# Moving a sign extraction from VectorE to ScalarE in the weight conversion of a fused attention and MLP kernel

## The chip, the cores and the metric

The kernel runs on one core of a Trainium2 chip. The core has TensorE (PE, matmuls and transposes into PSUM), VectorE (DVE), ScalarE (ACT), GpSimd (POOL) and SyncE (SP, which issues the DMAs here). The metric is the device time of one execution in microseconds (us).

## The reference

Three stages run one after another. A linear attention over 8 batches and 8 heads (576 positions, head size 64), then two MLPs over the 4608 resulting tokens of width 512:

```python
k_s = softmax(k, axis=2); q_s = softmax(q, axis=-1)
x = (q_s @ (k_s^T @ v)) as [4608, 512]
g = x @ w_gate; x = (silu(g) * (x @ w_val)) @ w_out      # hidden size 1536
h = x @ w_in;   x = elu(h) @ w_out2                       # hidden size 2048
```

The weights come as float64, the activations as float32.

## The kernel before, in words

Tokens are worked on in nine blocks of 512. Phase "a" runs the first MLP on one half of its hidden tiles (f, six tiles of 128) for all nine blocks, phase "b" on the other half, phase "2" runs the second MLP. During phase "a" the attention of the block after next is spread over the steps of the current block by hand-written plans (PLAN0, PLAN1, PLAN: name, then the pass f and step s at which it is issued). There is no reordering by a scheduler: every engine executes its instructions in the order in which the program issues them.

Every product is made of three matmuls over split operands: a high part and a low part of the weights and of the activations (mm3, proj). One pass over a hidden tile in phases "a" and "b" is gate (12 matmuls into a PSUM bank "a"), value (12 into the other bank "a"), and 12 matmuls of the output product of the pass before. Between them ACT computes parts of silu (L660 to L663), DVE multiplies (L667, L670, L673), ACT writes the high part of the result (L645) and DVE or POOL the low part (L651). There are two banks "a", so the gate of the next pass needs L670 of this one to have read its bank. In phase "2" the bank is freed by L688.

The weights arrive as the bits of float64 numbers, in 68 chunks of [128, 512]. Each chunk goes through four stages, each with a counter in `stage`:

- load (L125, L127): SP loads the 64-bit words into a raw buffer (three buffers, nine chunks at the start by borrowing two others).
- scale (`conv_scale`, L139): ACT reads the upper 32-bit word as a float32, multiplies by 2^-112 and writes cg (three buffers).
- bits (`conv_bits`): DVE makes the bits of a float32 from cg and the lower word. L154 shifts cg left by 3 and clears the sign, into a PSUM tile c; L157 takes the sign bit of cg and ORs it in; L161 ORs the top three bits of the lower word in and writes cd (four buffers).
- split (`conv_split`): ACT copies cd as the high part of the weight (L182), POOL subtracts to get the low part (L183). Twenty weight slots in a ring hold the result until the last block has used it.

`conv()` issues one step of each stage in the order split, bits, scale, load, load. It is called three times per pass in block ("a", 0), once per step in block ("a", 1) until 18 chunks are split, twice per pass in the last block of phases "a" and "b", otherwise once per pass or not at all where the ring is full. `limit` holds the loader at 18 chunks until late in phase "a". Three chunks are converted in `first_block` before the passes begin.

Names that the steps below use: km is the key maximum (L270 to L273 on DVE), transposed by PE at L280 and L293; ke the shifted and exponentiated keys (L310, L312, then ACT L315, L316), read by PE at L331; q is shifted on POOL at L360 and normalised at L378 in block 0, transposed at L390, copied by ACT at L398 and multiplied at L451; L299 is an ACT copy of the broadcast key maximum.

Of the kernel before, what the change touches and what calls it, by code (L numbers as in the profile page):

```python
# [7 lines left out]
FP32 = mybir.dt.float32  # L8
F32R = mybir.dt.float32r
U32 = mybir.dt.uint32  # L10
I64 = mybir.dt.int64
ACTF = mybir.ActivationFunctionType
ALU = mybir.AluOpType
AX = mybir.AxisListType
# [3 lines left out]
def kernel(  # L18
# [23 lines left out]
    nc = tc.nc  # L42
# [9 lines left out]
    NW1, NW2, NRAW, NCG, NCD = 20, 12, 3, 3, 4  # L52
# [5 lines left out]
    cv_p = ctx.enter_context(tc.tile_pool(name="cv", bufs=2))  # L58
# [43 lines left out]
    stage = {"load": 0, "scale": 0, "bits": 0, "split": 0}  # L102
    raws, gs, ds, loaded, calls, free = {}, {}, {}, {}, [0], [0]
# [5 lines left out]
    def early_raws():  # L109
        t = x_p.tile([128, 4, 512], I64, tag="x", name="xraw")  # L110
        u = ev_p.tile([128, 2, 512], I64, tag="ev", name="evraw")
        for n in range(6):
            early[NRAW + n] = t[:, n] if n < 4 else u[:, n - 4]

    def conv_load():
# [6 lines left out]
        _, src, cols = chunks[n]  # L122
        t = early.pop(n) if n in early else raw_p.tile([128, 512], I64, tag="raw", name="raw")
        if cols:
# [7 lines left out]

    def conv_scale(wait=0):
        n = stage["scale"]
        if n >= stage["load"] or n >= stage["bits"] + NCG or calls[0] < loaded[n] + wait:
            return
        stage["scale"] += 1
        g = cv_p.tile([128, 512], U32, tag="cg", name="cg", bufs=NCG)
        nc.scalar.activation(  # L139
            out=g.bitcast(FP32), in_=raws[n][:, :, 1].bitcast(FP32), func=ACTF.Copy,  # L140
            scale=2.0 ** -112,
        )
        gs[n] = g

    def conv_bits():
        n = stage["bits"]
        if n >= stage["scale"] or n >= free[0] + NCD:
            return  # L150
        stage["bits"] += 1
        g = gs.pop(n)
        s = ps_c.tile([128, 512], U32, tag="c", name="c")
        nc.vector.tensor_scalar(  # L154
            s, g, 3, 0x7FFFFFFF, op0=ALU.logical_shift_left, op1=ALU.bitwise_and
        )
        nc.vector.scalar_tensor_tensor(  # L157
            out=s, in0=g, scalar=0x80000000, in1=s, op0=ALU.bitwise_and, op1=ALU.bitwise_or
        )
        d = cv_p.tile([128, 512], U32, tag="cd", name="cd", bufs=NCD)  # L160
        nc.vector.scalar_tensor_tensor(  # L161
            out=d, in0=raws.pop(n)[:, :, 0], scalar=29, in1=s,
            op0=ALU.logical_shift_right, op1=ALU.bitwise_or,
        )
        ds[n] = d

    def conv_split(eng):
        n = stage["split"]
# [12 lines left out]
        df = ds.pop(n).bitcast(FP32)  # L181
        nc.scalar.activation(out=w[:, 0, :], in_=df, func=ACTF.Copy)  # L182
        eng.tensor_tensor(w[:, 1, :], df, w[:, 0, :].bitcast(FP32), op=ALU.subtract)  # L183
# [3 lines left out]
    def conv(eng=None, wait=2):  # L187
        calls[0] += 1
        free[0] = stage["split"]
        conv_split(eng or nc.gpsimd)  # L190
        conv_bits()
        conv_scale(wait)
        conv_load()
        conv_load()
# [94 lines left out]
    def k2(b):  # L289
# [7 lines left out]
        if b == 1:  # L297
            mb = at1.tile([128, H, D], FP32, tag="km", name="mb")
            nc.scalar.activation(out=mb, in_=m, func=ACTF.Copy)  # L299
            km_t[b] = mb  # L300
# [13 lines left out]
    def kexp(b):  # L314
        nc.scalar.activation(out=ke[:, 0:4], in_=ke[:, 0:4], func=ACTF.Exp)  # L315
        nc.scalar.activation(out=ke[0:NREST, 4], in_=ke[0:NREST, 4], func=ACTF.Exp)  # L316

# [44 lines left out]
    def qexp(t, n):  # L362
        x = q_t[t][:, 4 * n:4 * n + 4]
        nc.scalar.activation(out=x, in_=x, func=ACTF.Exp)

# [105 lines left out]
    def first_block():  # L471
# [103 lines left out]
        qexp(0, 1)  # L575
        qnorm(0, 0, nc.gpsimd)
        conv_scale()
        conv_scale()
        kv(0, 0, 1)
        qT(0, 0)  # L580
        qT(0, 2)
        qsum(0, 1)
        qnorm(0, 1, nc.gpsimd)
        kv(0, 1, 1)
        conv_bits()
        conv_split(nc.gpsimd)
        qT(0, 1)
# [5 lines left out]
        load_q(1)  # L593
        xT(0, 2, 0)
        conv_bits()
        conv_split(nc.gpsimd)
        xT(0, 2, 1)
# [340 lines left out]
    with tc.manual_schedule():  # L938
        nc.gpsimd.memset(ident, 1.0)
        nc.gpsimd.affine_select(  # L940
            out=ident, in_=ident, pattern=[[-1, 128]], compare_op=ALU.is_equal, fill=0.0,
# [39 lines left out]
```

## Time and profile before

| what | value |
|---|---|
| median of 3 runs | 1791.45 us (1791.27 to 1791.88) |
| the profiled execution's own time | 1792.23 us |
| its span, first to last instruction | 1790.5 us |
| PE busy | 1752.0 us, 98% |
| DVE busy | 924.9 us, 52% |
| ACT busy | 856.0 us, 48% |
| POOL busy | 173.1 us, 10% |
| mean granted clock of TensorE | 0.995 |

The busy shares are means over stages with different limits. "Idle before" in a row is the time for which the engine stood still just before that instruction, and "<-" names what ended it. Times in a timeline are counted from the span's start.

### The profile page before, as it was taken

The page shows a single profiled execution, that of the slowest core. Times are in us where ns is not written, and L with a number is a line of the kernel's source. Part 1 is how long each engine was busy: PE and PEld are TensorE (multiplying, and loading weights), DVE is VectorE, ACT ScalarE, POOL GpSimd, SP SyncE. Part 2 cuts the span into 40 slices and gives each one's busy share as a digit, 9 for nine tenths or more (in the row PEclk, how much of TensorE's full clock was granted, in tenths as well). Part 3 has the DMA queues.
Part 4 walks back from the last instruction along what each step waited for, and adds up shares of the span by engine and source line. Part 5 has one row for each costly group of instructions (what it writes and reads, how often), then busy time and mean ns, then how long its engine had stood idle before and what let it go on. Part 6 is the DMA issues. An engine that isn't in the chain of part 4 may idle for free.

```text
span 1790.5 us, 21046 instructions
## 1 busy us (share of the span) xinstructions
PE 1752.0 (98%) x8448; PEld 1433.3 (80%) x8448; DVE 924.9 (52%) x1383; ACT 856.0 (48%) x1466; POOL 173.1 (10%) x135
## 2 busy tenths in 40 slices
PE   6799999999999999999999999999999999999999
PEld 4577888888888888888888788888888888888887
DVE  6866567556577666534346744333433343334343
ACT  4563544534465454433334654444444444444444
POOL 3630000000022222111113300000000000000000
PEclk9899999999999999999999999999999999999999
DMA  9274534341255344433334401010101010101000
GB/s 273 80 228 102 147 100 124 105 114 65 78 192 176 129 171 168 165 118 118 118 118 164 174 3 71 1 71 1 71 1 71 1 71 1 71 1 71 1 24 24
DMA packets 103106, 169.13 MB, mean 94 GB/s; under 512 B 41696, under 2 KB 80608, under 8 KB 98528
## 3 DMA queue, kind: packets, MB, share of 16 engines
q1 hardware_dynamic: 103008, 167.79, 28.5%
q8 instruction: 66, 1.08, 0.3%
q14 instruction: 32, 0.26, 0.0%
HBM read 111.15 MB, written 56.62 MB: 94 GB/s over the span
## 4 chain that ended last, share of the span: by engine, by line
PE 90%; issue 2%; DVE 2%; POOL 2%; ACT 2%; DMA 1%; SPq 1%; POOLq 0%; DVEq 0%; ACTq 0%
PE a L632 17%; PE a L633 17%; PE a L636 17%; PE y L613 12%; PE y L615 12%; PE y L614 12%; POOL w L183 1%; PE t L451 1%; DMA ev<-in_v 1%; PE t L390 1%; SPq L242 0%; PE t L331 0%; PE c L331 0%; DMA xs<-x 0%; POOL ke L310 0%
## 5 line engine op out<-in xcount | busy, mean ns | idle before, releaser
L632 PE MATMUL a<-x,w 128*128 128x512 f32 x1432 | 562.8, 393 | 1.5 <-DVE th L688 1.2
L633 PE MATMUL a<-x,w 128*128 128x512 f32 x1432 | 558.9, 390 | 0.7 <-POOL x L463 0.7
L636 PE MATMUL a<-x,w 128*128 128x512 f32 x1432 | 382.8, 389 | 0.0
L645 ACT ACTIVATE g<-th 128x512 fp32r<-128x512 f32 x252 | 159.3, 632 | 442.4 <-DVE th L673 226.3
L632 PEld LDWEIGHTS a<-x,w 128*128 128x128 f32 x1432 | 269.8, 188 | 60.7 <-DVE th L688 2.0
L633 PEld LDWEIGHTS a<-x,w 128*128 128x128 f32 x1432 | 269.8, 188 | 56.2 <-POOL x L463 1.2
L636 PEld LDWEIGHTS a<-x,w 128*128 128x128 f32 x1432 | 268.8, 188 | 55.8
L685 DVE SCALAR_TENSOR_TENSOR th<-e,th 128x512 f32<-128x512 f32 x144 | 100.9, 701 | 356.6 <-ACT e L684 356.6
L651 DVE TENSOR_TENSOR g<-th,g 128x512 fp32r<-128x512 f32 x246 | 176.2, 716 | 136.7 <-ACT g L645 136.6
L613 PE MATMUL y<-w,g 128*128 128x512 f32 x576 | 224.1, 389 | 0.0
L615 PE MATMUL y<-w,g 128*128 128x512 f32 x576 | 224.1, 389 | 0.0
L614 PE MATMUL y<-w,g 128*128 128x512 f32 x576 | 224.1, 389 | 0.0
L667 DVE SCALAR_TENSOR_TENSOR th<-th,e 128x512 f32<-128x512 f32 x108 | 77.3, 715 | 274.6 <-ACT th L663 274.6
L682 ACT ACTIVATE e<-a 128x512 f32<-128x512 f32 x144 | 86.1, 598 | 183.4 <-PE a L636 183.4
L613 PE MATMUL y<-g,w 128*128 128x512 f32 x432 | 171.8, 398 | 0.0
L660 ACT ACTIVATE e<-a 128x512 f32<-128x512 f32 x107 | 64.1, 599 | 224.4 <-PE a L636 224.3
L614 PE MATMUL y<-g,w 128*128 128x512 f32 x432 | 169.0, 391 | 0.0
L615 PE MATMUL y<-g,w 128*128 128x512 f32 x432 | 169.0, 391 | 0.0
L183 POOL TENSOR_TENSOR w<-cd,w 128x512 fp32r<-128x512 f32 x68 | 91.6, 1349 | 624.8 <-ACT w L182 604.1
L613 PEld LDWEIGHTS y<-w,g 128*128 128x128 f32 x576 | 108.2, 188 | 22.6
L615 PEld LDWEIGHTS y<-w,g 128*128 128x128 f32 x576 | 108.1, 188 | 22.5
L614 PEld LDWEIGHTS y<-w,g 128*128 128x128 f32 x576 | 108.1, 188 | 22.3
(137 smaller groups left out, 1705.7 us busy)
## 6 DMA issues: line engine op xcount, KB each, us to landing
xs<-x SPq DMA_DIRECT2D x9, 2048.0 KB, 6.3
x<-xs SPq DMA_DIRECT2D x36, 512.0 KB, 6.2
ys<-yst SPq DMA_DIRECT2D x36, 512.0 KB, 3.7
x<-ys SPq DMA_DIRECT2D x36, 512.0 KB, 7.2
raw<-in_moe_w_out SPq DMA_DIRECT2D x26, 512.0 KB, 3.3
yp<-ev SPq DMA_DIRECT2D x9, 1024.0 KB, 4.0
ev<-yp SPq DMA_DIRECT2D x9, 1024.0 KB, 7.9
raw<-in_moe_w_in SPq DMA_DIRECT2D x16, 512.0 KB, 4.0
```

The costliest lines, as they stand in the source:

```text
L183: eng.tensor_tensor(w[:, 1, :], df, w[:, 0, :].bitcast(FP32), op=ALU.subtract)
L613: nc.tensor.matmul(out=ps, lhsT=wh, rhs=xh, start=first, stop=False)
L614: nc.tensor.matmul(out=ps, lhsT=wh, rhs=xl, start=False, stop=False)
L615: nc.tensor.matmul(out=ps, lhsT=wl, rhs=xh, start=False, stop=last)
L632: nc.tensor.matmul(out=ps, lhsT=wh, rhs=x[:, c, 0, :], start=(c == 0), stop=False)
L633: nc.tensor.matmul(out=ps, lhsT=wh, rhs=x[:, c, 1, :], start=False, stop=False)
L636: nc.tensor.matmul(out=ps, lhsT=wl, rhs=x[:, c, 0, :], start=False, stop=(c == KD - 1))
L645: nc.scalar.activation(out=gt[:, 0, :], in_=src, func=ACTF.Copy)
L651: (eng or nc.vector).tensor_tensor(gt[:, 1, :], src, gt[:, 0, :].bitcast(FP32), op=ALU.subtract)
L667: nc.vector.scalar_tensor_tensor(out=t, in0=t, scalar=1.0, in1=e, op0=ALU.add, op1=ALU.mult)
L682: nc.scalar.activation(out=e, in_=h, func=ACTF.Relu, scale=-1.0)
L685: nc.vector.scalar_tensor_tensor(out=t, in0=e, scalar=1.0, in1=t, op0=ALU.add, op1=ALU.mult)
```

## The change

ACT makes the sign as well. After L139 it issues a second activation on the same cg: Prelu with scale 2^90 and slope 2^100 for negative inputs, written as a 32-bit integer into cd. A positive weight gives 0, a negative one a value far below the integer range, which is written as the bit pattern of the sign. DVE then needs two operations per chunk: one that shifts cg left by 3 and ORs cd in (into the PSUM tile c), and L161 as before, which now overwrites cd. The buffer cd is taken at the scaling step, so `conv_scale` gets the limit on cd's four buffers that `conv_bits` had, counted from the split stage's current position.

```diff
@@ def conv_scale(wait=0):
-        if n >= stage["load"] or n >= stage["bits"] + NCG or calls[0] < loaded[n] + wait:
+        if n >= stage["load"] or n >= stage["bits"] + NCG or n >= stage["split"] + NCD or calls[0] < loaded[n] + wait:
             return
...
+        d = cv_p.tile([128, 512], U32, tag="cd", name="cd", bufs=NCD)
+        nc.scalar.activation(
+            out=d.bitcast(I32), in_=g.bitcast(FP32), func=ACTF.Prelu, scale=2.0 ** 90,
+            alpha=2.0 ** 100,
+        )
         gs[n] = g
+        ds[n] = d
@@ def conv_bits():
-        if n >= stage["scale"] or n >= free[0] + NCD:
+        if n >= stage["scale"]:
             return
...
         s = ps_c.tile([128, 512], U32, tag="c", name="c")
-        nc.vector.tensor_scalar(
-            s, g, 3, 0x7FFFFFFF, op0=ALU.logical_shift_left, op1=ALU.bitwise_and
-        )
+        d = ds[n]
         nc.vector.scalar_tensor_tensor(
-            out=s, in0=g, scalar=0x80000000, in1=s, op0=ALU.bitwise_and, op1=ALU.bitwise_or
-        )
-        d = cv_p.tile([128, 512], U32, tag="cd", name="cd", bufs=NCD)
+            out=s, in0=g, scalar=3, in1=d, op0=ALU.logical_shift_left, op1=ALU.bitwise_or
+        )
         nc.vector.scalar_tensor_tensor(
             out=d, in0=raws.pop(n)[:, :, 0], scalar=29, in1=s,
             op0=ALU.logical_shift_right, op1=ALU.bitwise_or,
         )
-        ds[n] = d
```

## Rows read from the trace of the kernel before

**Rows 1.** Stretches: length, busy us per engine (instructions), granted clock, DMA share, GB/s.

```profile
core 0: us, PE busy (x) PEld busy (x) DVE busy (x) ACT busy (x) POOL busy (x), PEclk, DMA share, GB/s
34.00:116.00 82.00, 65.73 (x349) 49.39 (x349) 63.92 (x91) 44.98 (x81) 48.80 (x35) 0.90 0.53 133
...
520.00:565.00 45.00, 45.00 (x200) 37.28 (x199) 37.79 (x55) 27.80 (x52) 14.11 (x11) 1.00 0.59 199
...
950.00:1040.00 90.00, 88.46 (x387) 72.01 (x386) 66.23 (x95) 54.85 (x98) 35.50 (x26) 1.00 0.48 170
```

**Rows 2.** PE's waits: waiting, waited for: us in total, times, longest.

```profile
PE t L280 <- DVE km L273: 7.6, 1, 7.6
PE t L331 <- ACT ke L315: 3.1, 1, 3.1
...
PE a L632 <- DVE th L688: 1.2, 2, 0.6
```

**Rows 3.** Groups by line and form: busy us, mean ns, idle before.

```profile
L683 ACT ACTIVATE th<-e 128x512 f32<-128x512 f32 x144 | 91.0, 632 | 4.6
...
L139 ACT ACTIVATE cg<-raw 128x512 f32<-128x512 f32 x62 | 40.7, 659 | 3.0 <-DMA raw<-in_moe_w_in 1.9 <-DMA raw<-in_moe_w_out 1.1
...
L946 ACT ACT_TABLE_LOAD x1 | 1.3, 1283 | 0.8 <-PEq L964 0.8
```

**Rows 4.** Durations of single lines: ns min/median/max, first and last start.

```profile
L157 DVE SCALAR_TENSOR_TENSOR c<-cg,c x68: 695/695/697, 24.4 to 1019.9; 128x512 uint32<-128x512 uint32 x68
...
L667 DVE SCALAR_TENSOR_TENSOR th<-th,e x108: 676/693/2011, 41.1 to 995.5; 128x512 f32<-128x512 f32 x108
```

**Rows 5.** Timeline of POOL and DVE at 82 us: start, duration, instruction.

```profile
82.47 1.91 POOL L378 TENSOR_TENSOR qn<-q,qr 128x1024 f32<-128x1024 f32 x1
...
82.91 2.01 DVE L667 SCALAR_TENSOR_TENSOR th<-th,e 128x512 f32<-128x512 f32 x1
```

**Rows 6.** Timeline of the first block, chunk 0's bits.

```profile
23.41 1.90 POOL L378 TENSOR_TENSOR qn<-q,qr 128x1024 f32<-128x1024 f32 x1 [0.58 <-DVE rs L340]
...
24.45 0.69 DVE L157 SCALAR_TENSOR_TENSOR c<-cg,c 128x512 uint32<-128x512 uint32 x1
...
25.18 0.69 DVE L161 SCALAR_TENSOR_TENSOR cd<-raw,c 128x512 uint32<-128x512 uint32 x1
```

**Rows 7.** Timeline of DVE ahead of PE's longest wait.

```profile
45.39 1.05 DVE L270 TENSOR_TENSOR km<-k 128x512 f32<-128x512 f32 x1
...
49.83 0.68 DVE L273 TENSOR_TENSOR km<-km,kr 64x512 f32<-64x512 f32 x1
```

**Rows 8.** Timeline of POOL and ACT, 60 to 76 us.

```profile
60.77 1.29 POOL L183 TENSOR_TENSOR w<-cd,w 128x512 fp32r<-128x512 f32 x1 [4.26 <-ACT w L182]
...
70.44 1.90 POOL L360 TENSOR_TENSOR q<-q,qr 128x1024 f32<-128x1024 f32 x1
...
73.34 1.89 ACT L315 ACTIVATE ke<-ke 128x2048 f32<-128x2048 f32 x1
```

**Rows 9.** Timeline of ACT, 86 to 93 us.

```profile
86.87 0.63 ACT L645 ACTIVATE g<-th 128x512 fp32r<-128x512 f32 x1 [5.33 <-DVE th L673]
...
92.09 0.59 ACT L398 ACTIVATE qT<-t 128x512 f32<-128x512 f32 x1
```

**Rows 10.** Timeline of one pass in the last block of phase "a".

```profile
541.59 0.63 ACT L182 ACTIVATE w<-cd 128x512 fp32r<-128x512 f32 x1 [0.40 <-DVE cd L161]
542.12 0.66 ACT L139 ACTIVATE cg<-raw 128x512 f32<-128x512 f32 x1
...
543.24 0.60 ACT L660 ACTIVATE e<-a 128x512 f32<-128x512 f32 x1 [0.46 <-PE a L636]
...
546.13 0.69 DVE L670 TENSOR_TENSOR th<-th,a 128x512 f32<-128x512 f32 x1
...
548.48 0.39 PE L632 MATMUL a<-x,w 128*128 128x512 f32 x1
```

**Rows 11.** Timeline near the end of phase "b".

```profile
985.45 0.68 ACT L139 ACTIVATE cg<-raw 128x512 f32<-128x512 f32 x1 [1.12 <-DMA raw<-in_moe_w_out]
...
989.62 0.50 PE L632 MATMUL a<-x,w 128*128 128x512 f32 x1 [0.34 <-DVE th L670]
```

More of the change, by code (lines that the diff above doesn't have):

```diff
@@ L11 @@
 I64 = mybir.dt.int64
+I32 = mybir.dt.int32
 ACTF = mybir.ActivationFunctionType
@@ L153, in conv_bits @@
         s = ps_c.tile([128, 512], U32, tag="c", name="c")
-        nc.vector.tensor_scalar(
-            s, g, 3, 0x7FFFFFFF, op0=ALU.logical_shift_left, op1=ALU.bitwise_and
-        )
-        nc.vector.scalar_tensor_tensor(
-            out=s, in0=g, scalar=0x80000000, in1=s, op0=ALU.bitwise_and, op1=ALU.bitwise_or
-        )
-        d = cv_p.tile([128, 512], U32, tag="cd", name="cd", bufs=NCD)
+        d = ds[n]
+        nc.vector.scalar_tensor_tensor(
+            out=s, in0=g, scalar=3, in1=d, op0=ALU.logical_shift_left, op1=ALU.bitwise_or
+        )
         nc.vector.scalar_tensor_tensor(
```

## The prediction

> **What bounds the kernel now.** I read the page first: TensorE (PE) is busy 98% of the span and carries 90% of the chain that ended last, so the change, which touches only ScalarE (ACT) and VectorE (DVE), can move the time only where PE stands still for them. The table of stretches shows where that is: in 34 to 116 us PE is busy for 65.7 of 82 us at a mean granted clock of 0.90, with DVE at 63.9, POOL at 48.8 and ACT at 45.0; in 520 to 565 PE never stops though DVE is at 37.8 of 45; in 950 to 1040 it loses 1.5 us [rows 1]. The list of PE's waits then names the holders: the largest single ones are 7.6 us for the key maximum on DVE (L273) and 3.1 us for the key exponent on ACT (L315); late in the run 1.2 us in two waits for L688 [rows 2]. So the first 18 of the 68 chunks (the loader's limit until late in the first phase) stand in a stretch where DVE, POOL and ACT pass work to each other without slack, and the other 50 mostly behind a full PE.
>
> **What the change does to each engine.** Removed per chunk: one DVE operation of L157's kind and size, 0.695 us [rows 4]; from its start to the next one's it is 0.73 (24.45 to 25.18) [rows 6], and I count 0.72. Over 18 early chunks that is 13 us of DVE. Added per chunk: one ACT activation. The trace has no Prelu and no integer output; the nearest row below is L683, 0.632 us, the nearest above L139 itself, 0.659 [rows 3]; a second activation that reads what the one before wrote starts about as late as that one lasts, so I take 0.66 and keep 0.53, the step from one activation to an independent next (541.59 to 542.12) [rows 10], as lower bound. Over 18 chunks: 10 to 12 us of ACT. No DMA moves. The cd buffer is now claimed by ACT at the scaling step, so ACT could wait for POOL's L183 of the chunk four before; by the early timeline that one has ended some 3 us earlier at the closest, so I cost it at nothing; without that room it would add up to one POOL operation, 1.3 us, to the ACT chain of step 5.
>
> **The lock.** The remaining first DVE operation changes its operands: before, each of the two operations had at most one input in SBUF (L154 reads g alone, L157 reads g and the PSUM tile). Now it reads g and d, both in SBUF, and so becomes like L667. L157 lasts 695 to 697 ns in all 68 cases, whatever POOL does; L667, the same operation and size with two SBUF inputs, lasts 676 to 2011 [rows 4]. The 2011 ns case shows why: POOL's L378 ran from 82.47 to 84.38, L667 started at 82.91 and ended at 84.92, 0.54 us behind POOL's end [rows 5]. So the new operation costs 0.69 us when POOL is idle and up to 1.9 when it meets a long POOL operation, and a POOL operation that starts behind it waits some 0.5. With POOL busy 60% of 34 to 116 us [rows 1], this takes back most of the 0.72.
>
> The Trainium skill ("SBUF — State Buffer", Who interferes with whom) calls this pair of engines' shared port an exclusive lock that a DVE instruction with two SBUF inputs contends for; the trace agrees with its 2.01 us. With this rule the early sum is the one below; were the port split by bandwidth instead, only a share of each overlap would be lost and the first rival below would be likelier.
>
> **The sum**, carried forward by hand from the timeline, engine by engine, with the durations above (each step is an estimate, good to about 0.5 us):
> 1. First block: chunk 0's new operation comes due at 23.7, behind L378 (23.41, 1.90 us). It ends at 25.9 where L157 ended at 25.14, and L161 (25.18) moves with it [rows 6]; on ACT the split's copy L182 and the transposed copy behind it follow late. Chunk 2's Prelu also stands ahead of an x copy. PE reaches its first full projections 0.6 us late.
> 2. 34 to 50.6: four chunks ahead of the key maximum save 2.9 us of DVE, less one lock behind L183, less the later start, less the maxima's own waits (L270 takes 1.05 where 0.69 is its step; behind it POOL's turns set the pace) [rows 7]. L273 ends about 0.8 us earlier than at 50.51. PE's 7.6 us wait [rows 2] shrinks by that.
> 3. 50.6 to 59: two more chunks, of which one meets a 1.9 us subtraction on POOL. Lead kept: 0.7.
> 4. 59 to 75.3: POOL is the chain here, from L183 (60.77) to the end of L360 (72.34), and ACT's L315 (73.34) behind it holds PE until 75.23 [rows 8]. Four new operations take turns between POOL's: about +0.5 each on POOL, and the Prelu ahead of the copy L299 costs the lead. Result: PE about 1.1 us later than before.
> 5. 75 to 93: ACT runs without a gap from L645 (86.87) to the copy L398 (92.09) that PE waits on next [rows 9]. Two Prelus stand in that stretch: +1.3, and its start is 0.6 late. PE's next product starts about 1.8 us later than before; after the 18th chunk nothing is added, and PE carries that offset.
> 6. 116 to 950: in 520 to 565 two chunks are converted per pass over a hidden tile. The first Prelu fits into the 0.40 us that L182 waited, with 0.26 over; the second adds 0.66; 0.46 of ACT's wait at L660 absorbs part [rows 10]. The remainder, at most 0.46 a pass over five passes, is 2.3 us, against 1.66 that L670 (ending 546.82) has before PE needs its bank (548.48) [rows 10]. I take nothing, with 0.6 as upper bound. Elsewhere one chunk a pass or none: nothing.
> 7. 950 to 1040: the last block again has two chunks a pass. At 985.45 ACT waits for a raw load, then scales, and L660 behind it makes PE wait 0.34 at 989.62 [rows 11]; a Prelu in between makes that 1.0. The next passes push the first L688 past its bank's need by about 0.5, and one of the two later waits for L688 [rows 2] grows by 0.35. Together +1.5.
>
> Sum: 1.8 + 1.5 = +3.3 us. The profiled execution took 1792.23 (span 1790.5); the median of the runs shown is 1791.45, 0.8 less. By the median the forecast is 1794.7, +0.18%. About 0.2%, or 3.6 us, is what a measurement of this kernel can tell from no change, so I forecast "same", close to its edge; its own range is 1790 to 1795.
>
> **Rivals.**
> *DVE's saving reaches PE (faster).* If the new operation finds POOL idle between 34 and 59 us, six chunks give 6 × 0.72 = 4.3 us on the chain to PE's wait that ends at 50.5 and to its next one, and the POOL chain starts that much earlier: 1791.45 − 4.3 = 1787.1. For it: DVE is the fullest of the three there, and that wait is the longest [rows 1, 2]. Against it: L667's locks. It decides if the key exponent (L315) starts before 70 us.
> *ACT becomes the bound (slower).* If Prelus also delay the second L398 by DVE's late L673 (start 1.4 late instead of 0.6, +0.8), and step 7's block runs at ACT's pace, 0.46 a pass over six passes = 2.8 in place of 1.5, the sum is +5.4 or more: 1796.9. For it: the gapless ACT stretch [rows 9]. It decides at 92 us and at 989 us.
> *A table switch (slower by far).* The trace has one load of activation tables, L946, 1.283 us [rows 3], for Copy, Exp, Tanh, Relu and Abs together. If Prelu needed another set, each chunk would switch there and back: 2 × 1.283 = 2.57 us on ACT, 46 us for the 18 early chunks, and some 5 us a pass in the two blocks with two chunks a pass, 61 over twelve: about 1890. Nothing in the trace shows it; five functions under one load speak against it.
> The Trainium skill ("ScalarE: Activation LUTs", What ACT_TABLE_LOAD costs) gives some 2.66 us a switch with its drain, by which the early part would be an estimated 96 us. Its list of a set's cheap fillers (Table sets: the hidden batching unit) does not name Prelu, and no run here shows it.
>
> **How the numbers follow.** Same as forecast 0.46; DVE's saving 0.15; ACT bound 0.35; table switch 0.04. Hence faster 0.15, same 0.46, slower 0.39. The range reaches to the first rival's time below, and above past the second's with its bounds added (0.6 of step 6, and some 3 us if each of steps 1 to 5 errs the same way): 1787 to 1800.5; the table switch stays outside.
>
> **What the profile after would show.** The new DVE operation's minimum near 690 ns and maximum near 1900, mean above 0.8 early; Prelu at 0.63 to 0.66; one table load only; L280 starting about 49.8; L331 near 76.4; the second L398 near 94; PE's late waits together some 3 us instead of 1.5. The prediction is wrong if L331 moves forward, if Prelu lasts longer than 0.7, if a second table load appears, or if the Prelu waits for cd's buffer behind POOL.

## The result and the profile after

The changed kernel takes 1808.95 us (1808.54 to 1809.73, 4 runs) against 1791.38 us (4 runs) of the kernel before: ratio 1.0097, 95% interval 1.0085 to 1.0109. The forecast was 1794.7 in a range of 1787 to 1800.5, so the time lies above the range, and the change is slower by more than the 0.2% within which the prediction counted "same". The profiled execution's span is 1807.2 us, 16.7 more than before. PE's granted clock is 0.995 in both as a mean over the span. In the changed kernel L139 stands at L140, L161 at L167, L182 at L187, L183 at L188, L645 at L650, L660 at L665, L670 at L675, L673 at L678, L688 at L693; the Prelu is L147 and the new DVE operation L164.

The groups of the new lines first (columns as in [rows 3]):

```profile
L164 DVE SCALAR_TENSOR_TENSOR c<-cg,cd 128x512 uint32<-128x512 uint32 x68 | 73.2, 1077 | 7.6 <-ACT cd L147 6.6
L147 ACT ACTIVATE cd<-cg 128x512 int32<-128x512 f32 x68 | 43.0, 632 | 18.5 <-POOL w L188 14.1 <-ACT cg L140 0.4
...
L951 ACT ACT_TABLE_LOAD x1 | 1.3, 1283 | 0.8 <-PEq L969 0.8
```

The last row is the only table load, so the Prelu needed no set of its own. The Prelu lasts 632 ns, as [rows 3] let one expect. The new fact stands at its end: ACT stood idle 18.5 us ahead of the Prelus, 14.1 of it ended by POOL's split L188. That is the wait for a cd buffer: fourteen waits, all behind 960 us. The stretches of [rows 1] again:

```profile
34.00:116.00 82.00, 65.24 (x348) 48.52 (x348) 56.25 (x74) 53.54 (x95) 50.50 (x34) 0.92 0.52 136
520.00:565.00 45.00, 44.31 (x190) 35.04 (x190) 31.92 (x40) 32.63 (x61) 16.33 (x11) 1.00 0.56 186
950.00:1040.00 90.00, 77.84 (x326) 61.37 (x325) 54.01 (x73) 54.60 (x98) 31.17 (x23) 0.98 0.41 144
```

DVE is relieved by 7.7 us early (63.92 to 56.25), and PE gains nothing from it. In 520 to 565 PE now stops for 0.69 us; in 950 to 1040 it is busy 77.84 us instead of 88.46. In PE's list of waits the two early ones shown are shorter than before (7.6 and 3.1 us [rows 2]), and those for L675 and L693 have grown, from 0.3 us for L670 and 1.2 us for L688 in the kernel before:

```profile
PE t L285 <- DVE km L278: 5.8, 1, 5.8
PE a L637 <- DVE th L675: 5.5, 5, 1.7
PE a L637 <- DVE th L693: 5.0, 3, 3.8
...
PE t L336 <- ACT ke L320: 2.4, 1, 2.4
```

To place the loss I use the evictions of the accumulators, which mark the stages. The rows give count, ns min/median/max, first and last start: ACT evicts phase "a", DVE phase "b", ACT a part of phase 2. Kernel before:

```profile
L716 ACT ACTIVATE ev<-y x36: 577/594/613, 121.8 to 565.9; 128x512 f32<-128x512 f32 x36
...
L721 DVE TENSOR_TENSOR ev<-y,ev x36: 680/682/685, 612.8 to 1007.4; 128x512 f32<-128x512 f32 x36
...
L763 ACT ACTIVATE ev<-y x18: 579/589/599, 1096.5 to 1785.5; 128x512 f32<-128x512 f32 x18
```

The changed kernel:

```profile
L721 ACT ACTIVATE ev<-y x36: 577/594/612, 121.5 to 569.7; 128x512 f32<-128x512 f32 x36
...
L726 DVE TENSOR_TENSOR ev<-y,ev x36: 680/682/685, 615.6 to 1020.9; 128x512 f32<-128x512 f32 x36
...
L768 ACT ACTIVATE ev<-y x18: 579/588/598, 1113.2 to 1802.2; 128x512 f32<-128x512 f32 x18
```

Up to the first eviction nothing is lost (-0.3). From there to the first of phase "b" it is 494.1 instead of 491.0 (+3.1), from there to phase 2's first 497.6 instead of 483.7 (+13.9: 10.7 within "b", 3.2 behind it), and phase 2's remainder is 689.0 in both. The sum is the 16.7 us. Both losses sit where chunks are converted two to a pass, in the last blocks of phases "a" and "b".

This is one pass of the last block of phase "b" (ACT, POOL and PE's first product):

```profile
984.32 0.58 ACT L665 ACTIVATE e<-a 128x512 f32<-128x512 f32 x1
...
987.92 0.50 PE L637 MATMUL a<-x,w 128*128 128x512 f32 x1 [1.66 <-DVE th L675]
...
988.69 0.63 ACT L650 ACTIVATE g<-th 128x512 fp32r<-128x512 f32 x1 [2.27 <-DVE th L678]
...
989.23 0.61 ACT L187 ACTIVATE w<-cd 128x512 fp32r<-128x512 f32 x1
...
989.75 0.65 ACT L140 ACTIVATE cg<-raw 128x512 f32<-128x512 f32 x1
...
989.92 1.29 POOL L188 TENSOR_TENSOR w<-cd,w 128x512 fp32r<-128x512 f32 x1 [6.18 <-ACT w L187]
...
991.25 0.63 ACT L147 ACTIVATE cd<-cg 128x512 int32<-128x512 f32 x1 [0.85 <-POOL w L188]
...
992.48 1.30 POOL L188 TENSOR_TENSOR w<-cd,w 128x512 fp32r<-128x512 f32 x1 [1.26 <-ACT w L187]
...
993.82 0.63 ACT L147 ACTIVATE cd<-cg 128x512 int32<-128x512 f32 x1 [0.86 <-POOL w L188]
...
994.35 0.58 ACT L665 ACTIVATE e<-a 128x512 f32<-128x512 f32 x1
```

In this block scaling runs exactly four chunks ahead of the split. The Prelu of chunk n therefore wants the buffer of chunk n-4, whose split POOL has only just begun (989.92). It stands 0.85 us, twice a pass, and the silu (L665) that PE waits for is queued behind it. From one L665 to the next it is 10.03 us, and PE stands 1.66 us. In the kernel before, L660 comes every 8.16 us in this block, until ACT waits for raw loads:

```profile
959.40 0.60 ACT L660 ACTIVATE e<-a 128x512 f32<-128x512 f32 x1 [2.09 <-PE a L636]
...
967.56 0.60 ACT L660 ACTIVATE e<-a 128x512 f32<-128x512 f32 x1 [1.52 <-PE a L636]
```

At the start of phase 2 POOL is held longer:

```profile
1025.58 3.08 POOL L736 TENSOR_TENSOR yst<-ev,yst 128x512 fp32r<-128x512 f32 x2 [5.25 <-ACT yst L735]
...
1028.63 1.28 POOL L188 TENSOR_TENSOR w<-cd,w 128x512 fp32r<-128x512 f32 x1
...
1029.94 0.63 ACT L147 ACTIVATE cd<-cg 128x512 int32<-128x512 f32 x1 [2.87 <-POOL w L188]
...
1033.88 0.50 PE L637 MATMUL a<-x,w 128*128 128x512 f32 x1 [3.82 <-DVE th L693]
```

One claim waits 2.87 us behind POOL's two splits of y, and PE stands 3.82 us for the elu behind it.

That wait costs more than its length, because PE's granted clock falls behind it. These are two matmuls of one form, behind the wait and one pass later, and the stretch 1036 to 1038 us (columns as in [rows 1]):

```profile
1035.56 0.63 PE L638 MATMUL a<-x,w 128*128 128x512 f32 x1
...
1041.32 0.39 PE L638 MATMUL a<-x,w 128*128 128x512 f32 x1
...
1036.00:1038.00 2.00, 2.00 (x6) 1.62 (x5) 0.72 (x2) 1.79 (x4) 2.00 (x2) 0.50 0.11 43
```

The granted clock there is 0.50, the lower of the two levels, against 1.00 before the wait. The 12 matmuls of the product behind the wait take 4.46 us (1033.88 to 1038.34), the 12 of the next 2.72 (1041.09 to 1043.81), so some 1.7 of the 3.2 us behind "b" are the clock's.

### The profile page after: what moved, and what is told of

It reads as the page before. It is cut to its first block, busy times and chain, and to the rows that moved or that the text cites. A ratio compares the mean times of both kernels' runs of the same rounds, so it can differ in the third digit from the quotient of the medians.

```text
span 1807.2 us, 21099 instructions
## 1 busy us (share of the span) xinstructions
PE 1757.1 (97%) x8448; PEld 1435.0 (79%) x8448; DVE 907.6 (50%) x1315; ACT 896.2 (50%) x1534; POOL 178.4 (10%) x135
## 5 line engine op out<-in xcount | busy, mean ns | idle before, releaser
L650 ACT ACTIVATE g<-th 128x512 fp32r<-128x512 f32 x252 | 159.3, 632 | 429.9 <-DVE th L678 216.4
L637 PEld LDWEIGHTS a<-x,w 128*128 128x128 f32 x1432 | 269.8, 188 | 76.3 <-DVE th L675 10.5
L656 DVE TENSOR_TENSOR g<-th,g 128x512 fp32r<-128x512 f32 x246 | 181.0, 736 | 136.7 <-ACT g L650 136.7
L665 ACT ACTIVATE e<-a 128x512 f32<-128x512 f32 x107 | 63.8, 596 | 204.2 <-PE a L641 204.2
L188 POOL TENSOR_TENSOR w<-cd,w 128x512 fp32r<-128x512 f32 x68 | 94.0, 1382 | 630.0 <-ACT w L187 609.4
```

The lines of the kernel that those rows point to most:

```text
L637: nc.tensor.matmul(out=ps, lhsT=wh, rhs=x[:, c, 0, :], start=(c == 0), stop=False)
L650: nc.scalar.activation(out=gt[:, 0, :], in_=src, func=ACTF.Copy)
L656: (eng or nc.vector).tensor_tensor(gt[:, 1, :], src, gt[:, 0, :].bitcast(FP32), op=ALU.subtract)
```

## Experiments

Three theories, called A, B and C in this order in the first expectations. **Claim**: the loss is ACT's wait for the cd buffer. **Loop**: the loss is the extra activation, which makes ACT's in-order round longer than PE's pass of 8.16 us. **Lock**: it is DVE's operation with two SBUF inputs, 1077 ns on average instead of 695 to 697 [rows 4]. All runs in one table; the last three columns are read from the eviction rows of one profiled execution as above (first of "a"; to the first of "b"; from there to the first of phase 2), and phase 2's remainder is 688.9 to 689.0 in all. The column first "a" carries nothing below some 2 us: sign_raw and sign_mixed run the same code up to there and differ by 2.2, and the first write of bd lies between 19.3 and 21.3 us. Differences "by the medians" are against the kernel before as it ran beside each kernel (1791.7 to 1791.9; for the changed kernel 1791.38).

| kernel | us | ratio [95%] | first "a" | to "b" | to 2 |
|---|---|---|---|---|---|
| before | 1791.4 | 1 | 121.8 | 491.0 | 483.7 |
| after | 1808.95 | 1.0097 [1.0085, 1.0109] | 121.5 | 494.1 | 497.6 |
| lim3 | 1798.98 | 1.0040 [1.0027, 1.0052] | 121.5 | 494.1 | 487.7 |
| sign_raw | 1797.25 | 1.0033 [1.0021, 1.0045] | 121.8 | 493.6 | 485.9 |
| act_only | 1799.93 | 1.0048 [1.0034, 1.0061] | 122.9 | 494.1 | 487.2 |
| dve_only | 1790.09 | 0.9992 [0.9983, 1.0001] | 121.1 | 490.9 | 483.9 |
| act_claim | 1811.9 | 1.0113 [1.0098, 1.0129] | 123.7 | 494.5 | 498.0 |
| act_half | 1795.68 | 1.0022 [1.0012, 1.0032] | 124.0 | 491.4 | 485.7 |
| act_two | 1816.27 | 1.0138 [1.0121, 1.0155] | 125.3 | 503.9 | 491.3 |
| sign_late | 1801.49 | 1.0056 [1.0041, 1.0071] | 130.7 | 490.9 | 483.8 |
| sign_mixed | 1792.68 | 1.0007 [0.9998, 1.0016] | 124.0 | 491.0 | 483.7 |
| claim_only | 1805.15 | 1.0076 [1.0062, 1.0090] | 120.5 | 491.0 | 497.8 |
| cd_late | 1793.14 | 1.0008 [0.9999, 1.0016] | 121.3 | 491.0 | 484.4 |
| dve_nolock | 1783.91 | 0.9961 [0.9948, 0.9974] | 114.2 | 491.0 | 482.3 |
| lock_three | 1798.64 | 1.0038 [1.0025, 1.0052] | 127.4 | 491.0 | 484.9 |
| sign_psum | 1798.12 | 1.0034 [1.0022, 1.0046] | 129.2 | 491.0 | 484.0 |
| sign_psum2 | 1793.16 | 1.0006 [0.9998, 1.0015] | 122.9 | 491.0 | 483.5 |

**lim3**: the changed kernel, scaling one chunk less far ahead.

```diff
-        ... or n >= stage["split"] + NCD or calls[0] < ...
+        ... or n >= stage["split"] + NCD - 1 or calls[0] < ...
```

> The changed kernel with one number lowered: scaling may run at most 3 chunks ahead of the split stage, not 4, so that the Prelu takes a cd buffer whose last reader was issued one conv call earlier. Theory A (the loss is ACT standing behind POOL for cd's buffer, twice a pass in the last block of phase b): the 0.85 us gaps before Prelu vanish, a pass there falls from 10.0 to at most 8.4 us, the time to 1791 to 1794 us. Theory B (one more activation per chunk already makes ACT's loop longer than PE's 8.16 us a pass): 1797 us or more. Theory C (DVE's two SBUF inputs meet POOL): unchanged, 1805 or more.

Ten of the 17 us come back, all of them behind the first eviction of "b" (497.6 to 487.7). No Prelu of that block waits for POOL any more, and its passes are 8.52 us (L650 at 966.89 and 975.41). But the time is in the range of B: the 3.1 us of phase "a" stay, and so do 4.0 behind it.

**sign_raw**: the sign goes into the upper words of the raw chunk, which nobody reads any more; cd is claimed by DVE as before, under the old limits.

```diff
+        nc.scalar.activation(out=raws[n][:, :, 1].bitcast(I32), in_=g.bitcast(FP32),
+            func=ACTF.Prelu, scale=2.0 ** 90, alpha=2.0 ** 100)
...
-            out=s, in0=g, scalar=3, in1=d, ...
+            out=s, in0=g, scalar=3, in1=raws[n][:, :, 1], ...
```

> The changed kernel with the sign written into the dead upper words of the raw chunk instead of into cd; cd is claimed by DVE in the bits stage again and both limits are those of the kernel before. The same ACT and DVE operations otherwise (Prelu writes and DVE reads at a stride of 8 bytes). Theory A: 1790 to 1793 us, no wait of the Prelu for POOL. Theory B: 1797 or more. Theory C: 1805 or more.

Without any claim by ACT 5.4 us stay by the medians: 2.6 in phase "a", 2.2 in the last column. There is a second cause.

**act_only**: the kernel before with that Prelu added, its result read by nobody.

```diff
+        nc.scalar.activation(out=raws[n][:, :, 1].bitcast(I32), in_=g.bitcast(FP32),
+            func=ACTF.Prelu, scale=2.0 ** 90, alpha=2.0 ** 100)
         gs[n] = g
```

> The kernel before with only the extra Prelu per chunk, into the dead upper words of the raw chunk, which nobody reads; DVE makes the bits in three operations as before. Theory A: 1791 to 1793.5 us (ACT's extra 0.65 us per chunk is nearly covered). Theory B: 1797 or more. Theory C: as before, 1791.

The extra activation alone costs 8.1 us by the medians, and 3.1 in phase "a", as much as the whole change does there. One round of ACT in the last block of "a":

```profile
535.34 0.63 ACT L650 ACTIVATE g<-th 128x512 fp32r<-128x512 f32 x1 [2.27 <-DVE th L678]
535.88 0.61 ACT L187 ACTIVATE w<-cd 128x512 fp32r<-128x512 f32 x1
536.40 0.66 ACT L140 ACTIVATE cg<-raw 128x512 f32<-128x512 f32 x1
537.08 0.68 ACT L144 ACTIVATE raw<-cg 128x512 int32<-128x512 f32 x1
...
539.42 0.59 ACT L665 ACTIVATE e<-a 128x512 f32<-128x512 f32 x1
...
543.80 0.63 ACT L650 ACTIVATE g<-th 128x512 fp32r<-128x512 f32 x1 [2.28 <-DVE th L678]
```

ACT is busy everywhere but in the 2.27 us in which DVE works on what ACT has just made for it (L668 to L650). That wait belongs to the round: 8.46 us from one L650 to the next, against PE's 8.16.

**dve_only**: DVE's two operations without a Prelu; the chunk is ORed with itself, so sign and mask are left out.

```diff
-        nc.vector.tensor_scalar(s, g, 3, 0x7FFFFFFF, ...)
...
-            out=s, in0=g, scalar=0x80000000, in1=s, ...
+            out=s, in0=g, scalar=3, in1=g, op0=ALU.logical_shift_left, op1=ALU.bitwise_or
```

> The kernel before with DVE's two operations only: no Prelu, cd claimed by DVE, old limits, and the shift ORed with the scaled word itself in place of the sign (both inputs in SBUF, so magnitudes are wrong and time alone is read). Theory A: 1789 to 1792 us. Theory B: 1788 to 1791. Theory C: 1800 or more, with new DVE operations of up to 1.9 us in the last block of phase b holding PE.

1.8 us faster by the medians, in an interval that includes no change. So DVE's two operations, lock included, make no loss against the kernel before. What the lock takes from the gain is asked below.

**act_half** and **act_two**: act_only with the Prelu on 256 of the 512 columns, and with two Prelus a chunk.

```diff
-            out=raws[n][:, :, 1].bitcast(I32), in_=g.bitcast(FP32), func=ACTF.Prelu,
+            out=raws[n][:, 0:256, 1].bitcast(I32), in_=g[:, 0:256].bitcast(FP32), func=ACTF.Prelu,
```

> As act_only (three operations on VectorE, a Prelu that nothing reads), but the Prelu covers 256 of the 512 columns, so about 0.35 to 0.4 us a chunk instead of 0.68. If the loss is ScalarE's in-order loop being longer than TensorE's pass (8.45 against 8.16 us in act_only, so 1.35 us of Prelu overshoot by 0.29), 0.75 us fit and the loss is nearly gone: 1791.5 to 1794. If every activation costs in proportion to its time wherever it stands: half of act_only's loss of 8.1 us, 1795 to 1797.

> As act_only with two Prelus a chunk. By the loop: a pass of 8.45 + 1.35 = 9.8 us in the ring-limited blocks, so each pass that act_only lengthened by 0.29 us is lengthened by 1.64 and others join: 1812 to 1825. By proportion: twice act_only's loss, about 1808.

In phase "a" the loop's threshold shows: +0.4 for half, +3.1 for one, +12.9 for two. With two a round is 9.86 us (L669 at 536.84 and 546.70), and the time is in the loop's range. In the median, though, half a Prelu costs 3.8 us, which is in the range of a cost in proportion and not in the loop's. By place 2.2 of it stand ahead of the first eviction, no more than the spread there, and 2.0 behind the first of "b", where the cost is nearly in proportion: 2.0, 3.5 and 7.6 us for half, one and two. The traces show why the loop's sum fails there. In one round of that block ACT waits for two raw loads, 1.88 us at 983.14 and 1.12 at 985.45 in the kernel before, and in act_half:

```profile
985.94 0.66 ACT L140 ACTIVATE cg<-raw 128x512 f32<-128x512 f32 x1 [2.10 <-DMA raw<-in_moe_w_in]
...
988.29 0.68 ACT L140 ACTIVATE cg<-raw 128x512 f32<-128x512 f32 x1 [0.72 <-DMA raw<-in_moe_w_out]
```

The loads have then used up the room. From the L660 ahead of them to the second behind them ACT takes 17.37 us in the kernel before (975.72 to 993.09) and 19.03 in act_half (978.29 to 997.32), which is 1.66 of the 2.0. No run took the load waits away, so this is read from the traces and not tested.

**claim_only**: the kernel before, no Prelu; the scaling itself writes into cd, claimed at scaling under the changed limit.

```diff
-        g = cv_p.tile([128, 512], U32, tag="cg", name="cg", bufs=NCG)
+        g = cv_p.tile([128, 512], U32, tag="cd", name="cd", bufs=NCD)
...
-        d = cv_p.tile([128, 512], U32, tag="cd", name="cd", bufs=NCD)
+        d = g
```

> Kernel before with its three operations on VectorE and no Prelu, but ScalarE's scaling writes straight into a cd buffer, claimed at scaling under the changed kernel's limit (split+4). If the claim's cost is a part of ScalarE's loop (7.27 us without the Prelu, plus two waits of some 1.4 to 1.5 us for GpSimd per pass of the last block of phase b, minus what scaling took: about 8.8 us against TensorE's 8.16), a third of the changed kernel's loss there: 1795 to 1799. If the claim costs its 10 us by itself: 1801 to 1803. If it costs only together with the Prelu: 1791 to 1793.

Above every expectation: 1805.15, and 14.1 us in the last column, the whole of the changed kernel's 13.9.

```profile
966.96 0.67 ACT L139 ACTIVATE cd<-raw 128x512 f32<-128x512 f32 x1 [1.41 <-POOL w L183]
...
969.56 0.67 ACT L139 ACTIVATE cd<-raw 128x512 f32<-128x512 f32 x1 [1.41 <-POOL w L183]
970.13 0.58 ACT L660 ACTIVATE e<-a 128x512 f32<-128x512 f32 x1
...
980.24 0.59 ACT L660 ACTIVATE e<-a 128x512 f32<-128x512 f32 x1
```

The expectation of 8.8 us a pass took the Prelu out of the round. But the first operation that writes cd stands behind POOL, here the scaling, and it waits 1.41 instead of 0.85. The pass is 10.11 us, against 10.03 in the changed kernel. In that block the claim sets the pass, and the Prelu on top is nearly free.

**act_claim**: three operations on DVE as before, and the Prelu into cd with the changed claim.

```diff
+        d = cv_p.tile([128, 512], U32, tag="cd", name="cd", bufs=NCD)
+        nc.scalar.activation(out=d.bitcast(I32), in_=g.bitcast(FP32), func=ACTF.Prelu, ...)
+        ds[n] = d
```

> VectorE keeps the three operations of before; ScalarE writes the Prelu into the cd buffer, which it takes at scaling under the changed kernel's limit (split+4); nothing reads the Prelu's words, VectorE writes over them. If the loss is the claim of the buffer (about 10 us) plus the extra activation (6 to 8 us), and VectorE's saving is worth under 2 us: 1806 to 1811, with two idle stretches of about 0.85 us before the Prelu in each pass of the last block of phase b. If VectorE's two longer operations have a part in the loss: at most 1802.

1811.9, just above its first range: the whole loss is there without DVE's change. The changed kernel is 3 us faster, but 2.2 of them stand ahead of the first eviction, within the spread there, so what DVE's two operations are worth is not shown by this pair.

**sign_late**: sign_raw with the Prelus issued behind the four activations of the next silu (or behind elu's), where ACT waits for DVE.

```diff
-        nc.scalar.activation(out=raws[n][:, :, 1].bitcast(I32), ...)
+        signs.append((raws[n], g))
...
         nc.scalar.activation(out=t, in_=t, func=ACTF.Abs)
+        flush_signs()
         return e, t
```

> As sign_raw (two operations on VectorE, the sign written over the dead upper words of the raw chunk, the buffer cd claimed by VectorE as before), but the Prelus are issued behind the four activations of the next silu, where ScalarE stands idle for about 2.2 us of a pass waiting for VectorE. If the loss of sign_raw (5.8 us) is the place of the extra activation in ScalarE's loop: gone, 1789 to 1793. If it is ScalarE's work as such, or VectorE's longer operation: 1796 to 1798 as in sign_raw.

1801.49 is above both ranges; the first theory holds by place. From the first eviction on it takes what the kernel before takes (490.9 and 483.8), so the same ACT work is free in the other place. Early on it loses 8.9 us: ahead of its first operation DVE stands 23 us for a sign made late, against 6 in sign_raw.

**sign_mixed** and **cd_late**: the late place only from the 18th chunk on; in cd_late the sign goes into cd, as in the changed kernel, and only the claim's place differs.

```diff
+        if n < 3 * HALF:
+            flush_signs()
```

> As sign_late, but the sign of the first 18 chunks is made at scaling (as in sign_raw), and only that of the later chunks behind the next silu or elu. In sign_late the steady blocks took what they take before (444.1 against 444.1 us over phase a's evictions, 395.7 against 394.6 over phase b's), and 8.9 us were lost ahead of the first eviction at 130.7 us, where bits and split stood waiting for a sign that came late. If both readings hold: 1801.5 - 8.9 = 1792.6, so 1790 to 1793.5. If the late place costs in the steady blocks too: 1795 or more.

> The changed kernel with its Prelu into the cd buffer, but for chunks from the 18th on the Prelu and its claim stand behind the next silu or elu (as in sign_mixed, with cd as the target). If the claim costs through the place at which ScalarE reaches it: GpSimd is done by then, and the time is that of sign_mixed, 1790 to 1796. If the claim itself costs: 1800 or more.

Both as expected where the place decides. cd_late shows that the claim is harmless at the late place. Its ACT still waits before one Prelu of a pass:

```profile
966.87 0.63 ACT L157 ACTIVATE cd<-cg 128x512 int32<-128x512 f32 x1 [1.34 <-POOL w L198]
...
967.96 0.58 ACT L675 ACTIVATE e<-a 128x512 f32<-128x512 f32 x1
...
969.95 0.63 ACT L157 ACTIVATE cd<-cg 128x512 int32<-128x512 f32 x1
```

**dve_nolock** and **lock_three**: the price of the two SBUF inputs. dve_nolock (the first edit) is dve_only with one input, the sign left out; lock_three (the second) puts two into the kernel before.

```diff
-            out=s, in0=g, scalar=3, in1=g, ...
+        nc.vector.tensor_scalar(s, g, 3, 0x7FFFFFFF, ...)
...
-            out=s, in0=g, scalar=0x80000000, in1=s, ...
+            out=s, in0=g, scalar=0x80000000, in1=g, ...
```

> As dve_only, but VectorE's first operation has one SBUF input instead of two (the OR of the chunk with itself is left out, so the words are wrong). If the longer operations of dve_only while GpSimd runs (1286 ns mean) cost at the end: 1787 to 1788.5, below dve_only's 1790.1. If they are hidden: within 0.7 us of dve_only, with a mean near 0.69 us for the operation.

> Kernel before with its three operations on VectorE, of which the second takes the chunk in SBUF as both inputs instead of the chunk and the PSUM tile (the words are then wrong, nothing else changes). If the two-input form costs by waiting for GpSimd (0.41 us more in each of the 18 early chunks, 7.3 us of VectorE's time ahead of phase a's first eviction): 1797 to 1799.5, the first eviction at 128 to 129 us instead of 121.8. If dve_nolock gained by something else: 1791 to 1793.

The operation in the first 122 us, in dve_only, dve_nolock and lock_three:

```profile
L154 DVE SCALAR_TENSOR_TENSOR c<-cg 128x512 uint32<-128x512 uint32 x18 | 20.2, 1124 | 3.2 <-ACT cg L139 2.7
```

```profile
L154 DVE TENSOR_SCALAR c<-cg 128x512 uint32<-128x512 uint32 x18 | 12.4, 689 | 3.5 <-ACT cg L139 3.1
```

```profile
L157 DVE SCALAR_TENSOR_TENSOR c<-cg 128x512 uint32<-128x512 uint32 x18 | 21.4, 1191 | 0.6
```

20.2 - 12.4 = 7.8 us of DVE, and 6.9 us in the first eviction (121.1 against 114.2). lock_three loses 6.7 us by the medians, in its first range. So one DVE operation less a chunk is worth 7.6 us ahead of the first eviction (121.8 to 114.2), and the two-input form takes 6.9 of them back (7.8 and 6.2 by the medians). dve_nolock's 1783.91 is below its first expectation (1787 to 1788.5).

**sign_psum** and **sign_psum2**: sign_mixed, but the early sign is written into the PSUM tile of the bits, so that DVE has one SBUF input; made just before the bits, or, in the second, behind the scaling where the tile is free.

```diff
+            nc.scalar.activation(out=s.bitcast(I32), in_=g.bitcast(FP32), func=ACTF.Prelu, ...)
...
-            out=s, in0=g, scalar=3, in1=raws[n][:, :, 1], ...
+            out=s, in0=g, scalar=3, in1=s, ...
```

> sign_mixed, but the sign of the first 18 chunks is written by ScalarE into the PSUM tile of the bits, just before VectorE's two operations, so the first of them has one SBUF input (about 0.70 us instead of 1.09). If the longer operation took back what VectorE saved: up to 6 us faster than sign_mixed, minus what VectorE waits for a sign made so late: 1785 to 1790. If the early stage stands on ScalarE: 1791 to 1794.

> As sign_psum, but the early sign is made right behind the scaling where the PSUM tile is free, so VectorE does not wait for it. By the first theory 1784.5 to 1788; by the second 1791 to 1794.

The lock is gone and the gain is not there: sign_psum is above both of its ranges, sign_psum2 in the second. The operation in sign_psum2, in the first 122 us:

```profile
L187 DVE SCALAR_TENSOR_TENSOR c<-cg,c 128x512 uint32<-128x512 uint32 x18 | 12.5, 692 | 11.9 <-ACT c L159 11.8
```

692 ns each, but DVE stands 11.8 us for the sign (27.2 in sign_psum): with one PSUM tile DVE and ACT now take turns. No version that makes every bit of the weights beat the kernel before; three equal it (sign_mixed, cd_late, sign_psum2).

## Why the prediction was wrong, point by point

- **The failed step: the cd buffer's claim, costed "at nothing"** with "up to one POOL operation, 1.3 us, to the ACT chain of step 5" as its bound. The reading ("some 3 us earlier at the closest") came from the early timeline, where no claim waited in the run either. In the last block of "b" the limit is reached on every chunk, and the claim alone costs 14.1 us there (claim_only). In the changed kernel some 1.7 of the 13.9 are the granted clock's, behind the longest wait. The prediction named this wait among what would make it wrong, but priced it once and not per pass, and not in steps 6 and 7.
- **Step 6, "I take nothing", at most 0.6**: +3.1 us, shown without any claim by act_only. The remainder per pass was right in kind and near in size: 0.37 (8.53 - 8.16 in the changed kernel) against "at most 0.46". The cover failed: five passes give 1.85, already above the 1.66 of [rows 10], and the pass at the block's entry, with the four evictions on ACT, was left out. It takes 8.99 us before and 10.42 in the changed kernel. From its start to the end of the block ACT takes 57.12 us before (to 567.72) and 61.73 after (to 572.02), 4.6 more, of which the cover of 1.66 leaves about 3. The entry pass before, then after:

```profile
510.60 0.60 ACT L660 ACTIVATE e<-a 128x512 f32<-128x512 f32 x1 [0.19 <-PE a L636]
...
519.59 0.62 ACT L660 ACTIVATE e<-a 128x512 f32<-128x512 f32 x1
```

```profile
510.29 0.60 ACT L665 ACTIVATE e<-a 128x512 f32<-128x512 f32 x1 [0.24 <-PE a L641]
...
520.71 0.58 ACT L665 ACTIVATE e<-a 128x512 f32<-128x512 f32 x1
```

- **Step 7, +1.5**: without the claim the Prelu costs 3.5 (act_only), 2.2 (sign_raw) or 4.0 us (lim3) in the last column, so the rival's 2.8 for "ACT becomes the bound" was the better size. The place was right: the raw load's wait leaves a Prelu no room. With the claim it is 13.9, and PE's waits for L675 and L693 come to 10.5 us where "some 3" were expected.
- **Steps 1 to 5, +1.8**: measured -0.3 at the first eviction, or about +0.7 if one allows for the first write of bd, which came at 20.02 instead of 21.04. With a spread of some 2 us there, no run tells this from +1.8 or from nothing. L285 starts at 48.31 (forecast 49.8), L336 at 74.64 (76.4), the second L403 at 91.92 (94). L331, now L336, did move forward from 75.29, which the prediction named as a sign of being wrong, but by less than the start did. The terms behind it were right in kind: the saving is 7.6, the lock takes 6.9; what the Prelus cost ACT there is not told apart from the spread. Of chunk 0 the forecast was exact but for that shift: the new operation met L383 and lasted 2.13 us (22.70 to 24.83), ending 0.55 behind POOL.
- **The lock** was right: 0.68 to 2.27 us (forecast 0.69 to 1.9), 1.09 on average early. The rule of the Trainium skill ("SBUF — State Buffer", Who interferes with whom), an exclusive lock for DVE's two-input form, agrees with chunk 0's operation, which ended only behind POOL's; lock_three's takes 1191 ns early against 695 to 697 for the same operation with one PSUM input.
- **The first rival** (DVE's saving reaches PE) failed by the lock, as the prediction held against it. Without the lock the saving is larger than the 4.3 us that it was given, but where the sign is made too, DVE waits for it (sign_psum2). **The table switch** did not occur; its terms, 46 and 61 us, give about 1898 and not 1890.
- **By sum**: -0.3 early, +3.1 from the loop in "a", +13.9 behind it, as much as the claim costs alone. The parts do not add, by the medians: Prelu alone +8.1, claim alone +13.4, both 20.0 (act_claim), the change with its cheaper DVE 17.6.

Open: whether half a Prelu's 2.0 us in the last column go with the load waits, and what a Prelu costs ahead of the first eviction. Two further cd buffers, or a tile of its own for the sign, were not tried.

## What to carry to other kernels

When a step takes a buffer earlier, count the distance to the buffer's last reader where the pipeline is fullest, not where it starts: with N buffers and a producer exactly N ahead, every claim waits for the reader issued a moment ago, and everything behind it on that in-order engine waits too. A round with room for more work may have none where it waits for a load. An engine at 50% can still set the pass; add up its round with the wait for its own results, and put extra work into that wait, where 0.68 us twice a pass cost nothing. Fewer DVE operations are worth little if the one that is left reads two SBUF inputs while GpSimd works.

## What the runs showed of the hardware that was not expected

A Prelu of 128x512 that writes integers lasts 632 ns on average into SBUF, 667 to 677 into every second word, and 591 to 600 ns into PSUM, and it shares the one table load of 1283 ns with Copy, Exp, Tanh, Relu and Abs. DVE's two-input operation lost 0.41 to 0.50 us on average to POOL in the first 122 us (1094 to 1191 ns against 689 to 696), and its longest in the changed kernel took 2.27 us. PE's granted clock fell to 0.50 behind a wait of 3.82 us, and 12 matmuls took 4.46 us instead of 2.72; in claim_only it fell to 0.50 as well, behind a wait of 3.3 us.
